# Windowed attention ahead of two expert layers: one chunk of 32 queries with its own 64 keys, in place of two chunks with a shared window of 96

## The chip, the core and the metric

The kernel runs on one core of a Trainium2 chip. Its time is the device time of one execution in microseconds (us). Matrix products run on TensorE (PE in the rows; PEld is its weight load), elementwise work on VectorE (DVE), ScalarE (ACT) and GpSimd (POOL), and transfers are issued by SyncE's queue (SP).

## The reference

Attention looks at a window: 32 queries share 16 keys before them, their own 32 and 8 behind them, and 8 memory keys that all chunks of a batch have. The result goes through two feed-forward layers.

```python
batch, n_heads, seq, head_dim = 4, 8, 768, 64
chunk, left_ctx, right_ctx = 32, 16, 8
for c in range(seq // chunk):
    l_start, r_end = max(0, c*32 - 16), min(seq, c*32 + 40)
    k_full = concat([mem_k, k[:, :, l_start:r_end]])      # 8 + up to 56 keys
    v_full = concat([mem_v, v[:, :, l_start:r_end]])
    scores = (q_c @ k_full.T) / sqrt(64); scores -= max(scores)
    a = exp(scores); out_c = (a / (sum(a) + 1e-9)) @ v_full
x = out.reshape(3072, 512)
x = softplus(x @ w_in) @ w_out                            # 512 -> 2048 -> 512
out = ((x @ w_a) * (x @ w_b)) @ w_out2                    # 512 -> 1536 -> 512
```

## The kernel before, in words

The 3072 tokens are eight tiles of 384. For each tile the attention output `x` is written as a sum of two fp32r halves (high and low), and the first layer walks over 16 slices of 128 hidden units: twelve matmuls into `ph` (L538), softplus on ACT (L544 to L546) and DVE (`g`, L548), the split of `g` (`g_..h` on ACT L525, `g_..l` on DVE L528), and twelve matmuls into `px` (L561), two slices behind. The second layer (L725, L748) follows behind all tiles.

Attention is put between these matmuls. Tile 0 is done before the first `ph`, as six `Block`s of 64 queries that are pipelined over rounds (11 to 37 us), while SP loads and ACT and DVE convert the weights (`raw` L116, `w` L127 and L130). Tiles 1 to 7 take three `Unit`s of 128 queries each (u = 3 to 23), placed between the matmuls of the tile before by a table of due slots. A unit's steps are

- `turn`: 32x32 transposes on DVE bring keys and queries to `kt` and `qt` (L410 to L413), and ACT copies the 8 memory keys behind them (L415);
- `scores`: 32 products of 64 queries with 96 keys (L429), on four 64x64 pieces of the array, into two PSUM banks `sc`;
- `soft`: per head a DVE custom operation (mask, scale, minimum; L379) and an ACT exp with its sum (L383); `norm` on POOL;
- `flip` and `flip2`: ten 32x32-block transposes on DVE (L447) into the one tile `af`;
- `values`: 16 products with contraction 96 on two array pieces, into one PSUM bank `pxa` (L476), each of them 64 queries;
- `place`: ACT copies `pxa` to the high half of `x` (L483), DVE subtracts it from `pxa` for the low half (L484).

Units 3 to 5 (tile 1) differ: their keys come packed from tile loads (scores in pieces of 88 and 8 columns, L304 and L305, or 96 at L302), and `flip_p` transposes on PE through two banks and two ACT copies (L465, L466). The `Block`s have the same steps (scores L302, PE transposes L355, values L363 into `pxb`, place L369 and L370).

`pxa`, `sc` and the transposes' banks take turns in one pool of two PSUM banks named "att": the second `sc` bank of a unit is the bank that the `pxa` two allocations earlier held, so it waits for the place that reads it. PE's, DVE's and SP's orders are written by hand; ACT's and POOL's are the scheduler's from tile 1 on. On SP, a transfer waits for the one eight issues ahead of it. A matmul record with fp32 operands stands twice in the trace for each product.

Of the kernel before, what the change touches and what calls it, by code (L numbers as in the profile page):

```python
# [50 lines left out]
def attn_moe_moe2(ctx: ExitStack, tc: tile.TileContext, q, k, v, mem_k, mem_v,  # L51
# [16 lines left out]
    KS = KB // 32  # L68
    NTILE = NT // TT
    KT = DM // P  # L70
    NF1 = F1 // P
# [80 lines left out]

    def consts():
        make_identity(nc, ident)
        for i, m in enumerate(masks):
            nc.vector.memset(m, NEG)
            for w in range(2):
                for c in range(2):
                    r = slice(QB * w + CH * c, QB * w + CH * c + CH)
                    lo = CH * c + (LC if (i == 3 or (i == 0 and w == 0)) and c == 0 else 0)  # L160
                    hi = CH * c + LC + CH + RC - (RC if (i == 2 and w == c == 1) else 0)
                    nc.vector.memset(m[r, lo:hi], 0.0)
                    nc.vector.memset(m[r, CTX:KB], 0.0)

    NP = TT // 32

# [34 lines left out]

    class Values:
        def __init__(self, name):
            self.v = ap.tile([KB, 2, H, D], F32, name=f"vn{name}")
            self.b = None

        def fetch(self, b, n):
            vv = v[b].rearrange("h s d -> s h d")
            go = nc.sync.dma_start
            for w in range(2):  # L210
                r0 = QU * n - LC + QB * w
                lo, hi = max(r0, 0), min(r0 + CTX, S)
                go(self.v[lo - r0:hi - r0, w], vv[lo:hi])
                if lo > r0:
                    go(self.v[0:lo - r0, w], vv[0:lo - r0])
                if hi < r0 + CTX:
                    go(self.v[hi - r0:CTX, w], vv[2 * hi - r0 - CTX:hi])
                if self.b != b:
                    go(self.v[CTX:KB, w], mem_v[b].rearrange("h m d -> m h d"))
            self.b = b  # L220

    mem_n = ap.tile([P, KT, 32], F32, name="mem_n")
# [6 lines left out]
    for x in (1, 3):  # L229
        nc.gpsimd.memset(af[0:32, x], 0.0)  # L230

    xt = {}

# [8 lines left out]
    class Packed:  # L242
# [66 lines left out]
    class Block:  # L309
# [9 lines left out]
        def load(self):  # L319
            u = self.u  # L320
            if u % 2 == 0:
                first["v"] = wp.tile([P, 2, H, D], F32, tag="w", name=f"vv{u}")
            self.vn = t = first["v"][:KB, u % 2]
            s0 = QB * u - LC
            lo = max(s0, 0)
            go = nc.sync.dma_start
            go(t[lo - s0:CTX], v[0, :, lo:s0 + CTX, :].rearrange("h s d -> s h d"))
            if lo > s0:
                go(t[0:lo - s0], v[0, :, 0:lo - s0, :].rearrange("h s d -> s h d"))
            go(t[CTX:KB], mem_v[0].rearrange("h m d -> m h d"))  # L330

        def scores(self):
            u = self.u
            work = wp.tile([P, 1024], F32, tag="w", name=f"work{u}")
            self.sm = work[:, :KT * KB].rearrange("p (i k) -> p i k", i=KT)
            self.st = work[:, KT * KB:KT * KB + 4 * KT].rearrange("p (n i) -> p n i", n=4)
            sc = self.psum(2, "scb")[:, :KT * KB].rearrange("p (i k) -> p i k", i=KT)
            for i in range(KT):
                for j in range(2):
                    r = slice(64 * j, 64 * j + 64)  # L340
                    packed[0].scores(sc[r, i], i, r, QB * u)
            self.sc = sc

        def soft(self):
# [4 lines left out]

        def flip(self):  # L350
            u = self.u
            self.af = wp.tile([KB, KT, P], F32, tag="w", name=f"afb{u}")
            pa = self.psum(3, "pat")[:KB, :].rearrange("p (i t) -> p i t", i=KT)
            for i in range(KT):
                nc.tensor.transpose(pa[:, i], self.sm[:, i], ident)  # L355
            nc.scalar.copy(self.af, pa)

        def values(self):
            self.px = px = self.psum(4, "pxb")[:, :KT * QB].rearrange("p (i t) -> p i t", i=KT)
            for i in range(KT):  # L360
                for j in range(2):
                    r = slice(64 * j, 64 * j + 64)
                    nc.tensor.matmul(px[r, i], lhsT=self.vn[:, 2 * i + j, :], rhs=self.af[:, i, r], start=True, stop=True)  # L363

        def place(self):
            u = self.u
            x = x_tile(0)
            xh, xl = x[:, 0, :, u * QB:u * QB + QB], x[:, 1, :, u * QB:u * QB + QB]
# [23 lines left out]
    class Unit:  # L392
# [10 lines left out]
        def turn(self):  # L403
            u, kn, qn = self.u, loaded.k, loaded.q
            n0 = 4 * (u % UPT)
            if self.n == 0:
                nc.vector.transpose(out=mem_t, in_=mem_n)
            self.kt = a2.tile([P, KT, 2, KB], F32, tag="kt", name=f"kt{u}", bufs=1)
            self.qt = a2.tile([P, KT, QU], F32, tag="qt", name=f"qt{u}", bufs=1)
            nc.vector.transpose(out=self.kt[:, :, :, :64].rearrange("p i w (m s) -> p i w m s", m=2),  # L410
                                in_=kn[:, :, n0:n0 + 4].rearrange("p i (w m) d -> p i w m d", m=2))
            nc.vector.transpose(out=self.kt[:, :, :, 64:], in_=kn[:, :, n0 + 2:n0 + 5:2])
            nc.vector.transpose(out=self.qt, in_=qn[:, :, n0:n0 + 4].rearrange("p i n d -> p i (n d)"))  # L413
            for w in range(2):
                nc.scalar.copy(self.kt[:, :, w, CTX:], mem_t[:, :, :M])  # L415

        def scores(self):
            u = self.u
# [2 lines left out]
            for i in range(KT):  # L421
                for j in range(2):
                    r = slice(64 * j, 64 * j + 64)
                    for w in range(2):
                        c = slice(QB * w, QB * w + QB)
                        if u < 2 * UPT:
                            packed[1].scores(self.sc[j][c, i], i, r, QU * (u - UPT) + QB * w)
                            continue
                        nc.tensor.matmul(self.sc[j][c, i], lhsT=self.qt[r, i, c], rhs=self.kt[r, i, w],  # L429
                                         start=True, stop=True)  # L430

        def soft(self):
# [9 lines left out]

        def flip(self, pieces=(0, 1)):

            for x in pieces:
                for kb in range(x % 2, KS):
                    nc.vector.transpose(out=af[32 * kb:32 * kb + 32, x],  # L447
                                        in_=self.sm[32 * x:32 * x + 32, :, 32 * kb:32 * kb + 32])

        def flip2(self):  # L450
            self.flip((2, 3))
# [7 lines left out]

        def flip_p(self):  # L460

            for j in range(2):
                pa = ps.tile([P, 512], F32, tag="att", name=f"pa{j}_{self.u}")[:KB].rearrange("p (i t) -> p i t", i=KT)
                for i in range(KT):
                    nc.tensor.transpose(pa[:, i], self.sm[:, KT * j + i], ident)  # L465
                nc.scalar.copy(af[:, :, KT * j:KT * j + KT], pa.rearrange("p i (x s) -> p x i s", x=4))  # L466

        def values(self):
            u = self.u
            vn = self.v.v  # L470
            self.px = px = ps.tile([P, 512], F32, tag="att", name=f"pxa{u}").rearrange("p (i t) -> p i t", i=KT)

            for w in range(2):
                for i in range(KT):
                    for j in range(2):
                        nc.tensor.matmul(px[64 * j:64 * j + 64, i, QB * w:QB * w + QB], lhsT=vn[:, w, 2 * i + j],  # L476
                                         rhs=af[:, 2 * w:2 * w + 2, KT * j + i], start=True, stop=True)

        def place(self):
            t, c0 = divmod(self.u * QU, TT)  # L480
            x = x_tile(t)
            xh, xl = x[:, 0, :, c0:c0 + QU], x[:, 1, :, c0:c0 + QU]
            nc.scalar.copy(xh, self.px)  # L483
            nc.vector.tensor_tensor(xl, self.px, xh.bitcast(F32), ALU.subtract)  # L484

    def warm(n, what=ident):

# [541 lines left out]
```

## Time and profile before

| | before |
|---|---|
| time, median of 3 runs (range) | 1198.33 us (1197.76 to 1199.57) |
| profiled execution | 1196.18 us, span 1194.1 us |
| PE busy | 1180.2 us (99% of the span) |
| PEld busy | 1120.6 us (94%) |
| DVE busy | 736.9 us (62%) |
| ACT busy | 536.3 us (45%) |
| POOL busy | 279.3 us (23%) |
| DMA | 209.86 MB, mean 176 GB/s |

The busy times are sums over the span; a PE that is 99% busy says that nearly every change on PE's path shows in the time, and that the others wait for it. The profiled execution lies 2.15 us below the median of the runs, 2.08 us of it outside the span.

### The profile page before, as it was taken

To read this page: it belongs to the slowest core of one execution; us is meant where nothing else is said; L and a number is where in the kernel's file an instruction comes from. 1 tells how busy PE (TensorE), PEld (TensorE's weight loads), DVE (VectorE), ACT (ScalarE), POOL (GpSimd) and SP (SyncE) were. 2 spreads that over 40 slices of the span, in tenths; PEclk is the share of its full clock that TensorE was granted. 3 is DMA by queue.
4 is the path that set the end of the run, shared out by engine and by line. 5 is a ranking of instruction groups with operands and counts; after the bars stand their busy time and mean duration, and the time that the engine had idled before them with its cause. 6 is when DMAs were issued, how large, how long until landed. Compare 5 with 4: busy or idle time off the path is not lost.

```text
span 1194.1 us, 21573 instructions
## 1 busy us (share of the span) xinstructions
PE 1180.2 (99%) x7994; PEld 1120.6 (94%) x7994; DVE 736.9 (62%) x1706; ACT 536.3 (45%) x1329; POOL 279.3 (23%) x249
## 2 busy tenths in 40 slices
PE   8999999999999999999999999999999999999998
PEld 8899999999999999999999999999999999999997
DVE  7888654556545565455387677755656456655565
ACT  6898656665566666566564433211112211212110
POOL 1000322323223222232325878200211002100000
PEclk9999999999999999999999999999999999999999
DMA  9955244352443534432465895788554965379521
GB/s 238 300 168 107 81 109 101 108 102 86 109 97 111 102 92 103 111 95 66 149 231 208 324 342 199 267 316 308 202 197 142 373 232 182 129 265 364 185 77 54
DMA packets 198697, 209.86 MB, mean 176 GB/s; under 512 B 121616, under 2 KB 149952, under 8 KB 198592
## 3 DMA queue, kind: packets, MB, share of 16 engines
q1 hardware_dynamic: 198208, 208.43, 54.7%
q8 instruction: 63, 1.03, 0.4%
q14 instruction: 42, 0.34, 0.1%
q0 software_dynamic: 384, 0.05, 0.0%
HBM read 158.11 MB, written 50.33 MB: 175 GB/s over the span
## 4 chain that ended last, share of the span: by engine, by line
PE 89%; DVE 3%; ACT 3%; DMA 2%; SPq 1%; issue 1%; DVEq 0%; ACTq 0%
PE ph L538 20%; PE px L561 20%; PE py L748 17%; PE pW L725 8%; PE pV L725 8%; PE pX L725 8%; PE pY L725 4%; PE pxa L476 2%; PE sc L429 1%; DMA kp<-in_k_dram 1%; DVE af L447 1%; DMA raw<-in_moe_w_in_dram 1%; ACT sm L383 1%; SPq L330 1%; DVE g L548 1%
## 5 line engine op out<-in xcount | busy, mean ns | idle before, releaser
L538 PE MATMUL ph<-x,w 128*128 128x384 f32 x1536 | 289.7, 336 | 0.1
L538 PEld LDWEIGHTS ph<-x,w 128*128 128x128 f32 x1536 | 267.0, 188 | 2.4 <-issue 0.3
L748 PE MATMUL py<-w2o,c 128*128 128x512 f32 x864 | 222.9, 394 | 0.7 <-DVE c L818 0.5
L548 DVE SCALAR_TENSOR_TENSOR g<-ph,e 128x384 f32<-128x384 f32 x128 | 71.3, 557 | 206.7 <-ACT e L546 198.8
L748 PEld LDWEIGHTS py<-w2o,c 128*128 128x128 f32 x864 | 159.9, 188 | 26.8 <-DVE c L818 1.1
L807 ACT CAST c<-c 128x384 fp32r<-128x384 f32 x48 | 24.7, 514 | 303.9 <-DVE c L805 271.2
L725 PE MATMUL pX<-x,u 128*128 128x384 f32 x576 | 115.5, 334 | 0.0
L757 DVE TENSOR_TENSOR y<-py,y 128x512 f32<-128x512 f32 x120 | 82.9, 691 | 48.2 <-PE py L748 47.8
L544 ACT ACTIVATE e<-ph 128x384 f32<-128x384 f32 x128 | 62.3, 486 | 102.3 <-PE ph L538 86.5
L725 PEld LDWEIGHTS pX<-x,u 128*128 128x128 f32 x576 | 102.1, 188 | 4.1
L447 DVE STREAM_TRANSPOSE af<-sm 32x256 f32<-32x256 f32 x180 | 78.2, 435 | 2.6
L545 ACT ACTIVATE e<-e 128x384 f32<-128x384 f32 x128 | 67.3, 526 | 4.0
L803 DVE TENSOR_TENSOR d<-pW,q 128x384 f32<-128x384 f32 x48 | 26.7, 557 | 68.4 <-PE pW L725 68.4
L546 ACT ACTIVATE e<-e 128x384 f32<-128x384 f32 x128 | 67.3, 526 | 3.7
L383 ACT ACTIVATE sm<-sm,st 128x96 f32<-128x96 f32 x168 | 60.5, 361 | 4.9 <-DVE st L379 4.9
L817 ACT CAST c<-c 128x384 fp32r<-128x384 f32 x48 | 24.6, 513 | 77.8 <-DVE c L815 76.9
L725 PE MATMUL pW<-xs,u 128*128 128x384 f32 x288 | 57.8, 335 | 0.0
L725 PE MATMUL pV<-xx,u 128*128 128x384 f32 x288 | 57.8, 335 | 0.0
L725 PE MATMUL pW<-xx,u 128*128 128x384 f32 x288 | 57.6, 334 | 0.0
L725 PE MATMUL pY<-xs,u 128*128 128x384 f32 x288 | 57.6, 334 | 0.0
L725 PE MATMUL pV<-xs,u 128*128 128x384 f32 x288 | 57.6, 334 | 0.0
L725 PEld LDWEIGHTS pV<-xx,u 128*128 128x128 f32 x288 | 51.5, 188 | 4.1
(251 smaller groups left out, 2240.0 us busy)
## 6 DMA issues: line engine op xcount, KB each, us to landing
u<-u_scratch SPq DMA_DIRECT2D x108, 512.0 KB
u_scratch<-u SPq DMA_DIRECT2D x36, 512.0 KB
w2o<-w2o_scratch SPq DMA_DIRECT2D x36, 512.0 KB
u<-u_scratch SPq DMA_DIRECT2D x36, 256.0 KB
raw<-in_moe_w_in_dram SPq DMA_DIRECT2D x16, 512.0 KB
raw<-in_moe_w_out_dram SPq DMA_DIRECT2D x16, 512.0 KB
vn<-in_v_dram SPq DMA_DIRECT2D x35, 176.0 KB
raw_a<-in_moe_w_a_dram SPq DMA_DIRECT2D x12, 512.0 KB
```

The lines of the kernel that those rows point to most:

```text
L383: nc.scalar.activation(sm[:, h], sm[:, h], AF.Exp, bias=st[:, 0, h:h + 1], scale=-1.0, accum_out=st[:, 1, h:h + 1])
L447: nc.vector.transpose(out=af[32 * kb:32 * kb + 32, x], in_=self.sm[32 * x:32 * x + 32, :, 32 * kb:32 * kb + 32])
L538: nc.tensor.matmul(ph, lhsT=a, rhs=c, start=n == 0, stop=n == 3 * KT - 1)
L544: nc.scalar.activation(e, ph, AF.Abs)
L545: nc.scalar.activation(e, e, AF.Exp, scale=-1.0)
L546: nc.scalar.activation(e, e, AF.Ln, bias=1.0)
L548: nc.vector.scalar_tensor_tensor(g, ph, 0.0, e, ALU.max, ALU.add)
L561: nc.tensor.matmul(acc[t][i][:, :TT], lhsT=a, rhs=c, start=f == 0 and m == 0, stop=f == NF1 - 1 and m == 2)
L725: nc.tensor.matmul(bank[:, :TT], lhsT=u[:, j, a, kt * P:kt * P + P], rhs=x[:, c, kt, :], start=first_ and m == 0, stop=m == 3 * KH - 1, sk ...
L748: nc.tensor.matmul(b, lhsT=c[:, x, r], rhs=w[:, y], start=n == 0, stop=n == 3 * GROUP - 1)
L757: tt(y, b, y, ALU.add)
L803: tt(d21, w[:, :TT], q, ALU.add)
```

## The change

Chunks of 32 queries get their own 56 keys and the 8 memory keys, 64 in all, where two chunks shared 88 and 8. A score product has 32 queries and 64 columns, on 64x32 pieces of the array, eight of them; a unit has 32 products instead of 16 (64 records instead of 32). A value product has contraction 64 in the upper or the lower half of the array and 32 queries; the halves go to two PSUM banks, `pxa` and `pxb`, and `place` is two copies and two subtractions of 256 columns instead of one each of 512. Values are loaded per chunk (56 rows) and so overlap more. The PE transposes become products with columns of the identity, into one bank. The masks lose most of their work, since a chunk's own window needs no hole.

```diff
-    CTX = QB + LC + RC
+    CTX = CH + LC + RC
     KB = CTX + M
+    NC = QU // CH
...
-            self.v = ap.tile([KB, 2, H, D], F32, name=f"vn{name}")
+            self.v = ap.tile([P, 2, H, D], F32, name=f"vn{name}")
...
-            for w in range(2):
-                r0 = QU * n - LC + QB * w
+            for g in range(NC):
+                x, y = divmod(g, 2)
+                r0 = QU * n - LC + CH * g
...
-    af = ap.tile([KB, 4, H, 32], F32, name="af")
+    af = ap.tile([P, H, 2, CH], F32, name="af")
...
-            lhsT = self.q[i][r, s0:s0 + QB]
+            lhsT = self.q[i][r, s0:s0 + CH]
...
-            go(t[lo - s0:CTX], v[0, :, lo:s0 + CTX, :].rearrange("h s d -> s h d"))
...
-            go(t[CTX:KB], mem_v[0].rearrange("h m d -> m h d"))
+            for c in range(2):
+                s0 = QB * u + CH * c - LC
...
+                go(t[to + lo:to + s0 + CTX], v[0, :, lo:s0 + CTX, :].rearrange("h s d -> s h d"))
...
+                go(t[KB * c + CTX:KB * c + KB], mem_v[0].rearrange("h m d -> m h d"))
...
-                nc.tensor.transpose(pa[:, i], self.sm[:, i], ident)
+                for c in range(2):
+                    nc.tensor.matmul(pa[KB * c:KB * c + KB, i], lhsT=self.sm[:, i], rhs=one[:, c], start=True, stop=True)
...
-            nc.vector.transpose(out=self.kt[:, :, :, :64].rearrange("p i w (m s) -> p i w m s", m=2),
-                                in_=kn[:, :, n0:n0 + 4].rearrange("p i (w m) d -> p i w m d", m=2))
-            nc.vector.transpose(out=self.kt[:, :, :, 64:], in_=kn[:, :, n0 + 2:n0 + 5:2])
+            for m in (1, 0):
+                nc.vector.transpose(out=self.kt[:, :, :, 32 * m:32 * m + 32], in_=kn[:, :, n0 + m:n0 + m + NC])
...
-            for w in range(2):
-                nc.scalar.copy(self.kt[:, :, w, CTX:], mem_t[:, :, :M])
+            nc.scalar.copy(self.kt[:, :, :, CTX:],
+                           mem_t[:, :, :M].rearrange("p i (o m) -> p i o m", o=1).to_broadcast([P, KT, NC, M]))
...
-                    for w in range(2):
-                        c = slice(QB * w, QB * w + QB)
+                    for g in range(NC):
+                        c = slice(CH * g, CH * g + CH)
...
-            for x in pieces:
-                for kb in range(x % 2, KS):
...
+            for g in pieces:
+                for kb in range(2):
...
-            for j in range(2):
-                pa = ps.tile([P, 512], F32, tag="att", name=f"pa{j}_{self.u}")[:KB].rearrange("p (i t) -> p i t", i=KT)
...
+            pa = ps.tile([P, 512], F32, tag="att", name=f"pa{self.u}").rearrange("p (h x s) -> p h x s", h=H, x=2)
...
-            self.px = px = ps.tile([P, 512], F32, tag="att", name=f"pxa{u}").rearrange("p (i t) -> p i t", i=KT)
...
+            self.px = [ps.tile([P, 512], F32, tag="att", name=f"px{'ab'[y]}{u}")[:, :KT * QB].rearrange(
+                "p (i x s) -> p i x s", i=KT, x=2) for y in range(2)]
...
-                        nc.tensor.matmul(px[64 * j:64 * j + 64, i, QB * w:QB * w + QB], lhsT=vn[:, w, 2 * i + j],
-                                         rhs=af[:, 2 * w:2 * w + 2, KT * j + i], start=True, stop=True)
+                    for y in range(2):
+                        k = slice(KB * y, KB * y + KB)
+                        for j in range(2):
+                            nc.tensor.matmul(self.px[y][64 * j:64 * j + 64, i, x], lhsT=vn[k, x, 2 * i + j],
+                                             rhs=af[k, KT * j + i, x], start=True, stop=True)
...
-            nc.scalar.copy(xh, self.px)
-            nc.vector.tensor_tensor(xl, self.px, xh.bitcast(F32), ALU.subtract)
+            x = x_tile(t)[:, :, :, c0:c0 + QU].rearrange("p n i (x y s) -> p n y i x s", x=2, y=2)
+            for y in range(2):
+                xh, xl = x[:, 0, y], x[:, 1, y]
+                nc.scalar.copy(xh, self.px[y])
+                nc.vector.tensor_tensor(xl, self.px[y], xh.bitcast(F32), ALU.subtract)
```

PE takes its blocks in the same order as before. Three places show how the other engines' orders move. The first is ACT around the place of unit 7, in tile 2's preparation, where `e_10` and `g_10h` belong to slice 10, `kt` to unit 8 and `raw_b` to a weight of the second layer. Before:

```order
217 L544 ACTIVATE e_10_2333<-ph_10_2320 128x384
218 L545 ACTIVATE e_10_2333<-e_10_2333 128x384
219 L415 COPY kt_2313<-mem_t 128x4x8 x2
220 L546 ACTIVATE e_10_2333<-e_10_2333 128x384
221 L483 CAST x_2093<-pxa_2343 128x4x128
222 L525 CAST g_10h<-g_10_2337 128x384
223 L635 ACTIVATE raw_b_2270<-raw_b_2270 128x512
224 L544 ACTIVATE e_11_2431<-ph_11_2418 128x384
```

And of the change, in the same place:

```order
224 L554 ACTIVATE e_10_2730<-ph_10_2717 128x384
225 L418 COPY kt_2711<-mem_t 128x16x8
226 L555 ACTIVATE e_10_2730<-e_10_2730 128x384
227 L556 ACTIVATE e_10_2730<-e_10_2730 128x384
228 L493 CAST x_2473<-pxa_2740 128x4x2x32
229 L535 CAST g_10h<-g_10_2734 128x384
230 L645 ACTIVATE raw_b_2669<-raw_b_2669 128x512
231 L493 CAST x_2473<-pxb_2741 128x4x2x32
232 L554 ACTIVATE e_11_2865<-ph_11_2852 128x384
```

The memory keys' copy stands ahead of two of the three softplus steps, and the second half of the place, from `pxb`, stands behind the split of `g` and a weight's conversion, not beside the first half.

The second place is DVE at the same point; `af` is the transposed softmax of unit 7. Before:

```order
373 L548 SCALAR_TENSOR_TENSOR g_9_2290<-ph_9_2273,e_9_2286 128x384
374 L447 STREAM_TRANSPOSE af<-sm_2151 32x256 x5
375 L410 STREAM_TRANSPOSE kt_2313<-kn 128x8x64
376 L412 STREAM_TRANSPOSE kt_2313<-kn 128x8x32
377 L413 STREAM_TRANSPOSE qt_2314<-qn 128x512
378 L548 SCALAR_TENSOR_TENSOR g_10_2337<-ph_10_2320,e_10_2333 128x384
379 L484 TENSOR_TENSOR x_2093<-pxa_2343,x_2093 128x4x128
```

And of the change:

```order
352 L558 SCALAR_TENSOR_TENSOR g_9_2689<-ph_9_2672,e_9_2685 128x384
353 L452 STREAM_TRANSPOSE af<-sm_2551 32x8x32 x4
354 L416 STREAM_TRANSPOSE kt_2711<-kn 128x16x32 x2
355 L417 STREAM_TRANSPOSE qt_2712<-qn 128x512
356 L558 SCALAR_TENSOR_TENSOR g_10_2734<-ph_10_2717,e_10_2730 128x384
357 L494 TENSOR_TENSOR x_2473<-pxa_2740,x_2473 128x4x2x32
358 L494 TENSOR_TENSOR x_2473<-pxb_2741,x_2473 128x4x2x32
```

One transpose of `af` less, a longer second `kt` transpose, and the one subtraction is two.

The third place is SP while the blocks' values and the first weights are loaded (`vv` are the values of blocks 2 and 3). Before:

```order
14 L101 DMA raw_155<-in_moe_w_in_dram 128x4x256
15 L327 DMA vv_157<-in_v_dram 88x8x64
16 L330 DMA vv_157<-in_mem_v_dram 8x8x64
17 L101 DMA raw_160<-in_moe_w_out_dram 128x1024
```

And of the change:

```order
18 L101 DMA raw_129<-in_moe_w_in_dram 128x4x256
19 L325 DMA vv_131<-in_v_dram 56x8x64
20 L328 DMA vv_131<-in_mem_v_dram 8x8x64
21 L325 DMA vv_131<-in_v_dram 56x8x64
22 L328 DMA vv_131<-in_mem_v_dram 8x8x64
23 L101 DMA raw_136<-in_moe_w_out_dram 128x1024
```

Between two weights four transfers of values stand where two stood, with 128 rows of 2 KB in place of 96.

## Rows read from the trace of the kernel before

**Rows 1.** The page: the chain that ended last, share by engine
```profile
PE 89%; DVE 3%; ACT 3%; DMA 2%; SPq 1%; issue 1%; DVEq 0%; ACTq 0%
```

**Rows 2.** Windows: PE, PEld, DVE, ACT, POOL busy, PEclk, DMA share, GB/s
```profile
16.00:22.00 6.00, 5.28 (x76) 4.70 (x75) 5.63 (x26) 5.11 (x22) 0.00 (x0) 1.00 1.00 238
...
93.00:97.00 4.00, 4.00 (x18) 3.60 (x16) 3.09 (x7) 3.61 (x7) 0.00 (x0) 0.57 0.77 183
```

**Rows 3.** The chain and ACT's timeline at the end of tile 0's attention
```profile
30.15 10.18 DMA raw<-in_moe_w_in_dram
...
40.35 0.71 ACT L116 ACTIVATE raw<-raw 128x512 f32<-128x512 f32 x1 [0.75 <-DMA raw<-in_moe_w_in_dram]
```

**Rows 4.** Timelines of ACT and PE at the end of tile 1's attention
```profile
90.89 1.04 ACT L466 COPY af<-pa 96x512 f32<-96x512 f32 x2
...
91.50 0.33 PE L476 MATMUL pxa<-af,vn 96*64 96x64 f32 x2 [1.34 <-ACT af L466]
91.99 1.15 PE L476 MATMUL pxa<-af,vn 96*64 96x64 f32 x30 [0.15 <-ACT af L466]
```

**Rows 5.** PE's timeline in a block's round
```profile
24.51 0.69 PE L363 MATMUL pxb<-afb,vv 96*64 96x64 f32 x16
...
25.77 0.88 PE L302 MATMUL scb<-kt,qt 64*64 64x96 f32 x16
```

**Rows 6.** PE's timeline, scores of unit 3 in pieces of 88 and 8 columns
```profile
53.21 0.40 PE L304 MATMUL sc<-kn,qn 64*64 64x88 f32 x8
53.40 0.28 PE L305 MATMUL sc<-kn,qn 64*64 64x8 f32 x8
53.48 0.41 PE L304 MATMUL sc<-kn,qn 64*64 64x88 f32 x8
```

**Rows 7.** PE's timeline, scores and values of two later units
```profile
198.73 0.89 PE L429 MATMUL sc<-kt,qt 64*64 64x96 f32 x32
...
218.48 1.15 PE L476 MATMUL pxa<-af,vn 96*64 96x64 f32 x32
```

**Rows 8.** Waits of PE: what for, us in total, times, longest us
```profile
PE pxa L476 <- DVE af L447: 1.6, 2, 1.1
...
PE sc L429 <- DVE x L484: 0.5, 1, 0.5
```

**Rows 9.** Timelines of PE, ACT and DVE around the place of unit 7
```profile
169.82 1.22 PE L476 MATMUL pxa<-af,vn 96*64 96x64 f32 x32
170.98 0.45 PE L561 MATMUL px<-g_8h,w 128*128 128x384 f32 x1
...
173.26 1.10 PE L429 MATMUL sc<-kt,qt 64*64 64x96 f32 x32
...
171.41 0.34 ACT L415 COPY kt<-mem_t 128x32 f32<-128x32 f32 x2 [0.43 <-DVE kt L412]
172.08 0.57 ACT L483 CAST x<-pxa 128x512 fp32r<-128x512 f32 x1
172.86 0.51 ACT L525 CAST g_10h<-g 128x384 fp32r<-128x384 f32 x1 [0.22 <-DVE g L548]
173.28 0.70 ACT L635 ACTIVATE raw_b<-raw_b 128x512 f32<-128x512 f32 x1
...
168.07 2.24 DVE L447 STREAM_TRANSPOSE af<-sm 32x256 f32<-32x256 f32 x5
170.34 0.71 DVE L410 STREAM_TRANSPOSE kt<-kn 128x512 f32<-128x512 f32 x1
170.97 0.40 DVE L412 STREAM_TRANSPOSE kt<-kn 128x256 f32<-128x256 f32 x1
172.75 0.68 DVE L484 TENSOR_TENSOR x<-pxa,x 128x512 fp32r<-128x512 f32 x1
```

**Rows 10.** ACT's and DVE's timelines: a block's place, of 256 columns
```profile
23.08 0.36 ACT L369 CAST x<-pxb 128x256 fp32r<-128x256 f32 x1
...
23.48 0.42 DVE L370 TENSOR_TENSOR x<-pxb,x 128x256 fp32r<-128x256 f32 x1
```

More of the change, by code (lines that the diff above doesn't have):

```diff
@@ L67, in attn_moe_moe2 @@
     BPT = TT // QB
-    KS = KB // 32
     NTILE = NT // TT
@@ L154, in consts @@
         make_identity(nc, ident)
-        for i, m in enumerate(masks):
-            nc.vector.memset(m, NEG)
-            for w in range(2):
[L158 to L163, printed above, removed]
+        for m in masks:
+            nc.vector.memset(m, 0.0)
+        for i, c in ((0, 0), (3, 0), (3, 2)):
+            nc.vector.memset(masks[i][CH * c:CH * c + CH, 0:LC], NEG)
+        nc.vector.memset(masks[2][QU - CH:QU, CTX - RC:CTX], NEG)
     NP = TT // 32
@@ L340, in scores @@
                     r = slice(64 * j, 64 * j + 64)
-                    packed[0].scores(sc[r, i], i, r, QB * u)
+                    for c in range(2):
+                        o = 64 * j + CH * c
+                        packed[0].scores(sc[o:o + CH, i], i, r, QB * u + CH * c)
             self.sc = sc
@@ L351, in flip @@
             u = self.u
-            self.af = wp.tile([KB, KT, P], F32, tag="w", name=f"afb{u}")
-            pa = self.psum(3, "pat")[:KB, :].rearrange("p (i t) -> p i t", i=KT)
+            self.af = wp.tile([P, KT, 2, CH], F32, tag="w", name=f"afb{u}")
+            pa = self.psum(3, "pat")[:, :KT * QB].rearrange("p (i j s) -> p i j s", i=KT, j=2)
+            one = ident.rearrange("p (j c s) -> p c j s", j=2, c=2)
             for i in range(KT):
-                nc.tensor.transpose(pa[:, i], self.sm[:, i], ident)
+                for c in range(2):
+                    nc.tensor.matmul(pa[KB * c:KB * c + KB, i], lhsT=self.sm[:, i], rhs=one[:, c], start=True, stop=True)
             nc.scalar.copy(self.af, pa)
         def values(self):
-            self.px = px = self.psum(4, "pxb")[:, :KT * QB].rearrange("p (i t) -> p i t", i=KT)
+            self.px = [self.psum(4, f"px{'ab'[c]}")[:, :KT * CH].rearrange("p (i t) -> p i t", i=KT) for c in range(2)]
             for i in range(KT):
-                for j in range(2):
-                    r = slice(64 * j, 64 * j + 64)
-                    nc.tensor.matmul(px[r, i], lhsT=self.vn[:, 2 * i + j, :], rhs=self.af[:, i, r], start=True, stop=True)
+                for c in range(2):
+                    k = slice(KB * c, KB * c + KB)
+                    for j in range(2):
+                        nc.tensor.matmul(self.px[c][64 * j:64 * j + 64, i], lhsT=self.vn[k, 2 * i + j, :],
+                                         rhs=self.af[k, i, j], start=True, stop=True)
         def place(self):
-            u = self.u
             x = x_tile(0)
-            xh, xl = x[:, 0, :, u * QB:u * QB + QB], x[:, 1, :, u * QB:u * QB + QB]
-            nc.scalar.copy(xh, self.px)
-            nc.vector.tensor_tensor(xl, self.px, xh.bitcast(F32), ALU.subtract)
+            for c in range(2):
+                s = QB * self.u + CH * c
+                xh, xl = x[:, 0, :, s:s + CH], x[:, 1, :, s:s + CH]
+                nc.scalar.copy(xh, self.px[c])
+                nc.vector.tensor_tensor(xl, self.px[c], xh.bitcast(F32), ALU.subtract)
     first = {}
@@ L423, in scores @@
                     r = slice(64 * j, 64 * j + 64)
-                    for w in range(2):
-                        c = slice(QB * w, QB * w + QB)
+                    for g in range(NC):
+                        c = slice(CH * g, CH * g + CH)
                         if u < 2 * UPT:
-                            packed[1].scores(self.sc[j][c, i], i, r, QU * (u - UPT) + QB * w)
+                            packed[1].scores(self.sc[j][c, i], i, r, QU * (u - UPT) + CH * g)
                             continue
-                        nc.tensor.matmul(self.sc[j][c, i], lhsT=self.qt[r, i, c], rhs=self.kt[r, i, w],
+                        nc.tensor.matmul(self.sc[j][c, i], lhsT=self.qt[r, i, c], rhs=self.kt[r, i, g],
                                          start=True, stop=True)
@@ L443, in flip @@
         def flip(self, pieces=(0, 1)):
-            for x in pieces:
-                for kb in range(x % 2, KS):
-                    nc.vector.transpose(out=af[32 * kb:32 * kb + 32, x],
-                                        in_=self.sm[32 * x:32 * x + 32, :, 32 * kb:32 * kb + 32])
+            for g in pieces:
+                for kb in range(2):
+                    o = KB * (g % 2) + 32 * kb
+                    nc.vector.transpose(out=af[o:o + 32, :, g // 2],
+                                        in_=self.sm[CH * g:CH * g + CH, :, 32 * kb:32 * kb + 32])
         def flip2(self):
@@ L460, in flip_p @@
         def flip_p(self):
-            for j in range(2):
-                pa = ps.tile([P, 512], F32, tag="att", name=f"pa{j}_{self.u}")[:KB].rearrange("p (i t) -> p i t", i=KT)
-                for i in range(KT):
-                    nc.tensor.transpose(pa[:, i], self.sm[:, KT * j + i], ident)
-                nc.scalar.copy(af[:, :, KT * j:KT * j + KT], pa.rearrange("p i (x s) -> p x i s", x=4))
+            pa = ps.tile([P, 512], F32, tag="att", name=f"pa{self.u}").rearrange("p (h x s) -> p h x s", h=H, x=2)
+            one = ident.rearrange("p (x y s) -> p y x s", x=2, y=2)
+            for h in range(H):
+                for y in range(2):
+                    nc.tensor.matmul(pa[KB * y:KB * y + KB, h], lhsT=self.sm[:, h], rhs=one[:, y], start=True, stop=True)
+            nc.scalar.copy(af, pa)
         def values(self):
```

32 lines of the change are left out of this document (14 added, 18 removed).

## The prediction

> **What bounds the kernel now.** I read the page's busy times first: PE is busy for 99% of the span. The chain that ended last puts 89% on PE and some 3% each on DVE and ACT [rows 1]; following it in order of time, that remainder lies in the first 98 us. Then the windows and timelines, stretch by stretch. Up to 37 us transfers fill the queue: 238 GB/s at a DMA share of 1.00, with no engine busy for the whole window [rows 2]; one transfer of weights holds 10.18 us of the chain, and behind it an ACT conversion stands 0.75 us for its weight [rows 3]. From there to 92 us ACT and DVE convert the remaining weights and do tile 1's softmax, and their chain ends where PE stands 1.34 us and then 0.15 for the two ACT copies of unit 5's transposes [rows 4]. Behind that the granted clock is 0.57 from 93 to 97 us [rows 2], nearer 1.2 than 2.4 GHz. From 98 us on PE itself is the bound: a step counts by what it occupies of PE, or by PE standing for it, and in the list of PE's waits little stands there [rows 8].
>
> **The price of a product.** 16 value records on two array pieces make a row of 0.69 us [rows 5], 32 a row of 1.15 [rows 7]: 0.46 us for eight more rounds, 58 ns for a round of 64 columns. Scores of 96 columns: 16 records on two pieces make 0.88 us [rows 5], 32 on four 0.89 [rows 7]. Twice the pieces did twice the work in the same time, and eight rounds of 96 columns cost 0.20 more than eight of 64, so a round of 96 takes 58 + 25 = 83 ns. Where rounds of 88 and of 8 columns alternate, two of each take 53.48 - 53.21 = 0.27 us [rows 6]; two of 88 columns, at 77 ns between the two prices, leave 0.12, 58 ns for a round of 8 columns. A round of few columns is no cheaper than one of 64.
>
> **Scores.** The change makes 64 records on eight pieces: eight rounds of 64 columns, 0.69 instead of 0.89 us, if eight run together as four did. That is -0.20 for each of 18 units (u = 6 to 23), **-3.6**. If only four run together, there are 16 rounds, 1.15, +0.26 each, +4.7. No row shows eight pieces; I take -3.6, for the doubling that rows do show was free.
>
> **Values.** A piece has eight products before and after, so 16 rounds, now of 32 columns on four pieces. At the 58 ns that 8 and 64 columns both cost: **0**. The bound below is half a round's price, -0.46 each, -8.3; the bound above is zero, since four pieces of this size do run together in the scores before [rows 7].
>
> **Values that wait for the flips.** Before, ten DVE transposes of 0.45 us each (five take 2.24 [rows 9]); now eight, so each half ends 0.45 earlier and both 0.9. PE stands for them twice, 1.6 us in all, 1.1 the longest [rows 8]: 0.9 and 0.5 of that go. Besides, 13 value blocks run 0.07 to 0.19 us over the 1.08 from their start to the next instruction (unit 7's: 169.82 to 170.98, 1.16 [rows 9]), 1.1 us in all, which go too. **-2.5**; bounds -2.7 and -1.4 (the short ones stay).
>
> **The place of units 7, 10 and 13.** These are the middle units of tiles 2, 3 and 4; here the next unit's scores come one `px` group behind the values, and their second bank is the one that the place must have read. Before, the scores row is 1.10 us instead of 0.89: PE stands 0.2 there already [rows 9]. Now: the flips end 0.45 earlier, and the second `kt` transpose takes 0.71 instead of 0.40, so ACT's memory copy, which waits for it, ends at about 171.45 instead of 171.65. But it now stands ahead of two softplus steps and not one, so the copy of `pxa` begins at about 172.45 instead of 172.08 [rows 9]. It takes 0.36 [rows 10] instead of 0.57, then come `g_10h` (173.2) and `raw_b` (173.6), since the copy of `pxb` was put behind both. With 0.57 us for `raw_b` from start to next start it begins at 174.2, takes 0.36; the subtraction adds 0.1 and 0.42 [rows 10]: 175.1. PE comes at 173.2. Queued behind its scores are the twelve `ph` matmuls of the next slice, whose softplus ACT and DVE take up next. PE stands 1.9 us less the 0.2 of before: 1.7 each, **+5.1**. Bounds: 0 if the copy of `pxb` finds ACT free earlier, +6 if the whole of `raw_b` is paid. In tiles 5 to 7 the order is the same, but the scores follow 5.5 us behind the values, which covers it. The 0.5 us of PE's other wait for a place [rows 8] belongs to unit 6 and stays.
>
> **The early transfers.** Six blocks load 64 KB more each, 384 KB; at 238 GB/s [rows 2] that is 1.65 us, and the 10.18 us transfer [rows 3] ends so much later, which ACT's conversion at 40.35 pays in full, as it stands for its weight already. I take **+1.7**; bounds 0 (if the transfers before had slack) and +3.4 (if many small rows cost twice). Within the blocks' rounds two short chains take the place of one, two PSUM banks are asked for instead of one, and DVE has some 0.2 us less per round; this ends in front of the last weight, which covers it.
>
> **From 46 to 98 us.** Sixteen exps lose 32 columns at (0.57 - 0.36)/256 us a column [rows 9, 10], -0.4; one copy of transposes instead of two, -0.5 (half of 1.04 [rows 4]); places in two pieces, +0.2: PE gets its values 0.7 earlier. The second half's wait with the split it makes, 91.50 to 91.99 [rows 4], is gone, -0.5, and unit 6's scores are 0.2 shorter. The PE transposes as 16 products have 16 rounds, +0.3, under PE's waiting. **-1.4**; bounds -3.1 (if the clock's fall, which cost about 1.7, goes as well) and 0.
>
> **What costs nothing.** Masks are set before the first load lands; POOL, 23% busy, normalises a third fewer columns; SP's additional loads from tile 2 on lie under a DMA share far from 1.
>
> **Sum.** -3.6 + 0 - 2.5 + 5.1 + 1.7 - 1.4 = -0.7: 1196.18 - 0.7 = 1195.5 for a profiled execution. The profiled one lies 2.15 below the median of the runs, so **1197.6** there. 0.2%, 2.4 us, is about what a measurement of this kernel can tell from no change.
>
> **Rivals.** *The clock falls after the new waits.* After the standing of 1.34 us at 91.5 the granted clock went to 0.57 [rows 2, 4]; after the one of 1.1 us in [rows 8] it stayed at full. Three standings of 1.9 us could each do it, at 1.7 us more: -0.7 + 3.4 = +2.7 for two, +4.4 for three, 1201.0 to 1202.7, slower. It decides from two falls on.
>
> *The place wait does not come about:* -0.7 - 5.1 = -5.8, 1192.5, faster. For it: PE is late by other work, or ACT is ahead by then. Against: ACT's order is fixed, and the replay above has 1.9 us to lose.
>
> *Eight pieces do not run together:* +0.46 x 18 = +8.3, 1205.9, slower. Against: four did.
>
> *Value products of 32 columns are cheaper than 58 ns:* -8.3, 1189.3, faster. Against: 8 columns cost as much as 64 [rows 6].
>
> *The early transfers are covered:* -1.7, 1195.9, at the bound of faster.
>
> *Evacuation is the price, not the order.* Every later unit pays two copies and two subtractions: (2 x 0.36 - 0.57) + (2 x 0.42 - 0.68) = 0.31 us [rows 9, 10], 18 times, 5.6 in place of 5.1: 1198.1. The Trainium skill, "TensorEngine Tiling (Array Packing)", section "PSUM Bottleneck", says that tiling speeds TensorE up but not the emptying of PSUM, and advises one access over several tiles of a bank; this change goes against that advice. The trace speaks against its price here: ACT is 45% busy and DVE 62%.
>
> **How the numbers follow.** The sum as it stands 0.38, the clock 0.17, no place wait 0.15, eight pieces apart 0.08, cheap values 0.08, transfers covered or evacuation 0.14. Faster: 0.15 + 0.08 + 0.07 of the transfers + 0.03 of the sum = 0.33; slower: 0.17 + 0.08 + 0.02 = 0.27; same 0.40. The range takes in the clock's three falls and the missing place wait, 1192.3 to 1202.7, and leaves out both array cases, 0.16. The likeliest case's own range is 1195.5 to 1200.
>
> **What would show it.** Right: scores of a later unit as a row of about 0.69 us; values 1.15; PE standing some 1.9 us before the second half of the scores near 173, 247 and 322 us, put down to the subtraction L494; ACT's conversion near 41 us standing longer than 0.75; the two waits for the flips shrunk. Wrong: a scores row above 1 us without a wait, values near 0.7, a granted clock below 1.00 after 98 us, or places that PE does not wait for.

## The result, and the profile after

The change is slower: 1205.76 us, median of 9 runs (1202.49 to 1210.22), against 1199.49 for the kernel before (9 runs, 1197.76 to 1200.36). The ratio is 1.0056, with a 95% interval of 1.0039 to 1.0073, so 5 to 9 us. Forecast were 1197.6 and no difference, with a range up to 1202.7. The profiled execution took 1202.49 us, its span is 1200.6, 6.5 above that of before. One execution of one kernel below, twice, took 3146 us at a granted clock of 1.00, with PE's products more than twice as long throughout, and is left out of its ratio.

The page: busy times, the chain's shares and, of the queue that the trace names "instruction", packets, MB and share.

```profile
PE 1183.5 (99%) x9866; PEld 1121.0 (93%) x9866; DVE 717.2 (60%) x1669; ACT 530.9 (44%) x1335; POOL 270.8 (23%) x247
...
PE 92%; ACT 3%; DVE 3%; issue 1%; DVEq 0%; POOL 0%; POOLq 0%
...
q8 instruction: 78, 1.28, 0.5%
```

DVE, ACT and POOL all have less to do than before, and PE is busy for only 3.3 us more, 2.3 of them in `ph` (292.0 against 289.7 us), whose matmuls are as many as before; the rows on the end of each tile show a wait inside them. The other 3.2 us are PE idle. Transfers have gone from the chain [rows 1]. So most of the 6.5 us is PE standing, and not more work. PE's waits, with what for, us in total, times and the longest:

```profile
PE scb L300 <- issue: 4.4, 3, 3.1
PE sc L433 <- DVE x L494: 3.4, 4, 1.0
PE sc L300 <- DVE x L494: 1.6, 1, 1.6
```

The waits for the flips [rows 8] are gone, and two kinds have grown: scores of the blocks that wait for nothing the profile shows ("issue"), and scores that wait for a place. A third kind stands only in the list of PE's weight loads, below.

To see where the time comes in, I set the same pieces of PE's order side by side in both traces. The first `ph` begins at 41.53 instead of 37.41, 4.1 later; at the first `ph` behind unit 5's scores (101.73 against 98.57) it is 3.2; behind the last unit's values, 6.9; at the end 6.5. So the first 40 us lose 4.1, the stretch from there to 100 us gives back 1.0, and tiles 1 to 6 lose 3.8.

**The first 40 us.** PE's timeline in the scores of block 1, in two later places, and the first `ph`:

```profile
13.03 0.25 PE L301 MATMUL scb<-kt,qt 64*32 64x8 f32 x5
16.35 0.27 PE L300 MATMUL scb<-kt,qt 64*32 64x56 f32 x4 [3.08 <-issue]
...
26.21 0.27 PE L300 MATMUL scb<-kt,qt 64*32 64x56 f32 x4 [0.80 <-issue]
...
36.07 0.24 PE L366 MATMUL pxa<-afb,vv 64*64 64x32 f32 x1 [0.36 <-issue]
...
41.53 2.61 PE L548 MATMUL ph<-x,w 128*128 128x384 f32 x12
```

And in the kernel before:

```profile
15.70 0.17 PE L305 MATMUL scb<-kt,qt 64*64 64x8 f32 x1 [0.77 <-issue]
...
37.41 2.66 PE L538 MATMUL ph<-x,w 128*128 128x384 f32 x12
```

The 3.08 us stand in the middle of block 1's scores, between two products of like operands. The kernel before stands for "issue" in the same stretch too, but 0.77 us. Behind the change's standing the granted clock is near 1.2 GHz for 4 us, which the kernel before does not have there (1.00 from 13 to 30 us); PE's windows of the change (length, PE busy, granted clock, DMA share, GB/s):

```profile
17.00:19.00 2.00, 2.00 (x68) 0.59 0.90 197
19.00:21.00 2.00, 2.00 (x12) 0.56 0.95 276
21.00:24.00 3.00, 3.00 (x112) 1.00 0.99 260
```

**The end of each tile.** ACT, DVE, PE and PE's weight loads where unit 8's place and the first `ph` of tile 2 meet (unit 8 is the last of that tile):

```profile
200.07 0.51 ACT L535 CAST g_15h<-g 128x384 fp32r<-128x384 f32 x1 [0.69 <-DVE g L558]
200.49 0.37 ACT L493 CAST x<-pxa 128x256 fp32r<-128x256 f32 x1
200.75 0.38 ACT L493 CAST x<-pxb 128x256 fp32r<-128x256 f32 x1
...
201.23 0.41 DVE L494 TENSOR_TENSOR x<-pxb,x 128x256 fp32r<-128x256 f32 x1
...
201.18 2.70 PE L548 MATMUL ph<-x,w 128*128 128x384 f32 x12
...
201.18 0.19 PEld L548 LDWEIGHTS ph<-x,w 128*128 128x128 f32 x1 [0.41 <-ACT x L493]
201.70 1.34 PEld L548 LDWEIGHTS ph<-x,w 128*128 128x128 f32 x8 [0.33 <-DVE x L494]
```

The next tile's `ph` reads all of `x`. It waits first for the copy, then for the subtraction. By the starts of the blocks on PE this costs 0.7 us in each of the six tiles 2 to 7: 0.25 in front of the `ph` and 0.46 inside its row. In the kernel before the copy of `pxa` stood ahead of `g_15h`, and the same `ph` took 2.25 us and waited for nothing:

```profile
194.83 0.57 ACT L483 CAST x<-pxa 128x512 fp32r<-128x512 f32 x1
195.62 0.51 ACT L525 CAST g_15h<-g 128x384 fp32r<-128x384 f32 x1 [0.22 <-DVE g L548]
...
196.56 2.25 PE L538 MATMUL ph<-x,w 128*128 128x384 f32 x12
```

**The place of unit 7,** and scores of a later unit that waits for nothing:

```profile
174.20 0.30 ACT L418 COPY kt<-mem_t 128x128 f32<-128x128 f32 x1 [0.23 <-DVE kt L416]
...
175.39 0.35 ACT L493 CAST x<-pxa 128x256 fp32r<-128x256 f32 x1
...
176.59 0.67 ACT L645 ACTIVATE raw_b<-raw_b 128x512 f32<-128x512 f32 x1
177.16 0.35 ACT L493 CAST x<-pxb 128x256 fp32r<-128x256 f32 x1
...
176.73 0.32 PE L433 MATMUL sc<-kt,qt 64*32 64x64 f32 x8
178.02 0.79 PE L433 MATMUL sc<-kt,qt 64*32 64x64 f32 x56 [0.98 <-DVE x L494]
...
203.81 0.86 PE L433 MATMUL sc<-kt,qt 64*32 64x64 f32 x64
204.60 0.44 PE L571 MATMUL px<-g_14h,w 128*128 128x384 f32 x1
```

The wait that the prediction replayed is there, in units 7, 10 and 13, but it is 0.98 long, and 1.29 from the first of the scores, where the replay had 1.9. And the 64 records of a unit's scores (32 products) take 0.79 us to the next instruction, hardly less than the 0.82 of the 32 records (16 products) before.

### The profile page after: what moved, and what is told of

It is laid out like the page before. It is cut to its first block, busy times and chain, and to the rows that moved or that the text cites. A ratio compares the mean times of both kernels' runs of the same rounds, so it can differ in the third digit from the quotient of the medians.

```text
span 1200.6 us, 25431 instructions
## 1 busy us (share of the span) xinstructions
PE 1183.5 (99%) x9866; PEld 1121.0 (93%) x9866; DVE 717.2 (60%) x1669; ACT 530.9 (44%) x1335; POOL 270.8 (23%) x247
## 4 chain that ended last, share of the span: by engine, by line
PE 92%; ACT 3%; DVE 3%; issue 1%; DVEq 0%; POOL 0%; POOLq 0%
PE ph L548 21%; PE px L571 19%; PE py L758 17%; PE pV L735 8%; PE pW L735 8%; PE pX L735 8%; PE pY L735 4%; PE sc L433 1%; PE fill L502 1%; DVE g L558 1%; ACT e L556 1%; ACT e L555 1%; PE pxa L485 1%; DVE af L452 1%; ACT e L554 1%
## 5 line engine op out<-in xcount | busy, mean ns | idle before, releaser
L548 PE MATMUL ph<-x,w 128*128 128x384 f32 x1536 | 292.0, 337 | 1.0
L767 DVE TENSOR_TENSOR y<-py,y 128x512 f32<-128x512 f32 x120 | 82.8, 690 | 48.6 <-PE py L758 48.2
L452 DVE STREAM_TRANSPOSE af<-sm 32x256 f32<-32x256 f32 x144 | 62.6, 435 | 2.7
L388 ACT ACTIVATE sm<-sm,st 128x64 f32<-128x64 f32 x168 | 56.0, 335 | 4.5 <-DVE st L384 4.5
```

The lines of the kernel that those rows point to most:

```text
L388: nc.scalar.activation(sm[:, h], sm[:, h], AF.Exp, bias=st[:, 0, h:h + 1], scale=-1.0, accum_out=st[:, 1, h:h + 1])
L452: nc.vector.transpose(out=af[o:o + 32, :, g // 2], in_=self.sm[CH * g:CH * g + CH, :, 32 * kb:32 * kb + 32])
L548: nc.tensor.matmul(ph, lhsT=a, rhs=c, start=n == 0, stop=n == 3 * KT - 1)
L767: tt(y, b, y, ALU.add)
```

## The experiments

Spans are those of the profiled executions, ratios those of the timed runs to the kernel before. Two theories stood against each other at each end. For the first 40 us: PE waits for its own longer instruction stream; or the larger value loads delay the blocks. For the rest: ACT's new order; or the price of emptying two banks, wherever it stands.

**place_first.** ACT takes a unit's two copies ahead of the split of `g`; the weight conversions (`raw_b`) that are due there are held back behind the split:

```diff
-                    emit_soft(t, f, ph)
+                    emit_soft(t, f, ph, place=partial(att_at, 2 * (NF1 * t + f)))
...
+            place()
+            copy = placed.pop()
+            with tc.issue_after(copy.ins) if copy else ExitStack():
+                gt[t, f] = split(g, f"g{t}_{f}", engine, two)
```

> The changed kernel, with the two copies of a unit's place put on ACT ahead of the split of the slice's g, as in the kernel before; PE's and DVE's orders stay. Theory (ACT's order costs the time from 98 us on): the first ph of tiles 2 to 7 no longer stands some 0.6 us for the place of the last unit, and the scores behind units 7, 10 and 13 stand some 0.6 us instead of 1.2: 6 x 0.6 + 3 x 0.6 = 5.4 us off, span about 1195 instead of 1200.6. The first 98 us stay as long as in the changed kernel. Rival (emptying two banks costs 0.3 us a unit wherever it stands): at most 1 us off.

Span 1195.4, 5.2 less than the change's, and ratio 1.0002 (0.9986 to 1.0018), 6.5 us less by the ratios. ACT and PE at the same two places:

```profile
199.63 0.36 ACT L493 CAST x<-pxa 128x256 fp32r<-128x256 f32 x1
199.88 0.38 ACT L493 CAST x<-pxb 128x256 fp32r<-128x256 f32 x1
200.42 0.52 ACT L537 CAST g_15h<-g 128x384 fp32r<-128x384 f32 x1 [0.16 <-DVE g L562]
...
201.28 2.24 PE L550 MATMUL ph<-x,w 128*128 128x384 f32 x12
...
178.24 0.92 PE L433 MATMUL sc<-kt,qt 64*32 64x64 f32 x64
```

The `ph` is back at 2.24 us, and the scores behind unit 7 stand 0.06 us instead of 0.98 + 0.25. The evacuation is as long as in the change; only ACT's order is another. So the order is the cause, and the price of the evacuation is out as a rival.

**old_blocks** and **both.** The six blocks of tile 0 as in the kernel before (64 queries, masks of 96 columns), in the change and in place_first:

```diff
+    CTXB = QB + LC + RC
+    KBB = CTXB + M
...
+                    packed[0].scores(sc[r, i], i, r, QB * u, QB)
```

> The changed kernel, with the six blocks of tile 0 as before: 64 queries, 96 keys, values loaded as 88 and 8 rows. Theory (the first 98 us lose time because PE stands for its own longer instruction stream in the blocks' scores): the first ph begins 3 to 4 us earlier than in the changed kernel and the span is about 1197. Rival (the blocks' end is covered by the weights' transfers, and the loss is in units 3 to 5): less than 1 us off.

> Both edits, place first and the old blocks. If the two losses are separate, the sum: 5.4 + 3.5 = 8.9 us off the changed kernel, span about 1191.5, some 2.5 us below the kernel before. If they overlap, or the shorter stretch meets another wait, between 1193 and 1196.

old_blocks: span 1197.8, first `ph` at 37.88, ratio 1.0022 (1.0013 to 1.0031), 4.1 us less than the change. both: span 1192.2, ratio 0.9966 (0.9956 to 0.9977). By the ratios the two edits take off 6.5 and 4.1 us alone and 10.8 together: two separate losses, as the sum of the two theories had it, and together they are more than all that the change lost. What is left of the change gains some 4 us.

**fewer_loads, one_product, loads, twice** take the blocks' loss apart: transfers or instructions.

```diff
 # fewer_loads, of the change
+            nc.gpsimd.memset(t[KB:P], 0.0)
-            for c in range(2):
+            for c in range(1):
 # one_product, of the change
-            if s0 + CTX == m0:
+            if s0 + CTX == m0 or self.t == 0:
 # loads, of the kernel before
+            go(more[:24], v[0, :, QB * u:QB * u + 24, :].rearrange("h s d -> s h d"))
+            go(more[24:], mem_v[0].rearrange("h m d -> m h d"))
 # twice, of the kernel before
+                    for _ in range(2):
                         packed[0].scores(sc[r, i], i, r, QB * u)
```

> The changed kernel, with no value loads for the second chunk of each block: those rows are zeros written by GpSimd, so half of tile 0's values are left out. Fewer bytes and no more transfers than in the kernel before, the PE instructions of the changed kernel. Instruction stream: the standing of about 3 us near 13 to 16 us stays, and the first ph begins at 40.5 us or later. Transfers: the first ph goes back to 37.5 to 38.5 and the span falls by 3 us or more.

> The changed kernel, with one score product of 64 columns a head and chunk in tile 0, where 56 and 8 columns take two: the 8 memory keys are left out there and the next 8 tokens stand in their place. The transfers of the changed kernel, 96 products fewer on PE ahead of the first ph. Instruction stream: the standing near 13 us falls below 1.5 us, and the first ph begins at 39 us or before. Transfers: the first ph stays at 41 us or later.

> The kernel before, with 24 and 8 rows of values more per block loaded to rows that nothing reads: the transfers' number and bytes of the changed kernel's blocks, PE as before. Theory (instruction stream): the first ph stays within 0.5 us of 37.4 and the span within 1 us. Rival (the value loads delay the blocks): the first ph 3 to 4 us later. The sum of the prediction has 1.7 later, at the weights' conversion behind 40 us.

> The kernel before, with each score product of the six blocks issued twice into the same columns: as many PE instructions there as in the changed kernel, same transfers, same values. Theory (PE stands for its own longer instruction stream in the blocks): a standing put down to no engine of 2 to 3 us near 11 to 16 us, and the first ph begins 3 to 4 us later than 37.4. Rival (the larger value loads delay the blocks): the first ph moves by the products' own 1.0 us or less, most of it covered.

> The kernel before with the blocks' score products issued twice, once more for its profile, since the first one was taken in an execution of 3146 us in which PE's products took more than twice as long throughout. Instruction stream: a standing put down to no engine of 2 to 3 us near 11 to 16 us, and the first ph 3 to 4 us later than 37.4. Transfers: 38.5 us or before.

PE's timelines of fewer_loads (two rows) and of one_product (one):

```profile
15.87 0.32 PE L300 MATMUL scb<-kt,qt 64*32 64x56 f32 x3 [3.09 <-issue]
...
28.31 0.19 PE L301 MATMUL scb<-kt,qt 64*32 64x8 f32 x1 [2.00 <-issue]
```

```profile
15.45 0.31 PE L298 MATMUL scb<-kt,qt 64*32 64x64 f32 x6 [1.08 <-issue]
```

With fewer bytes than before the standing is still 3.09 us; with the bytes of the change and fewer products (88 by the records) it falls to 1.08, and the first `ph` begins at 38.38. So the standing goes with PE's instructions, not with the value loads. fewer_loads' own time says nothing on the loads: after its two standings the granted clock was 0.59 from 30 to 45 us, its first `ph` came at 48.2, and its ratio is 1.0087.

one_product shows the transfers as well. Its ratio, 1.0043 (1.0028 to 1.0058), is hardly better than the change's: of the 3.2 us that it is ahead at the first `ph` 1.7 are lost at once, where ACT waits 2.02 us for a weight and PE 1.56 for the query copy behind it:

```profile
42.49 0.71 ACT L116 ACTIVATE raw<-raw 128x512 f32<-128x512 f32 x1 [2.02 <-DMA raw<-in_moe_w_in_dram]
...
48.52 0.88 PE L289 MATMUL ptq<-ident,qp 128*64 128x128 f32 x12 [1.56 <-DVE qn L291]
```

Of the rest, part goes near 61 us, where PE stands 0.64 us for "issue" again, and part in a fall of the clock (0.50 from 102 to 105 us) that the change's execution does not have, so its span does not give the sum.

loads: the first `ph` begins at 41.58, as the rival had it, while PE stands for "issue" only twice, 0.96 us at 9.5 (in the transposes of the keys) and 0.57 in the blocks. But the profiled execution is the longest of its ten runs, 1203.83 us; the shortest is 1197.94, and the ratio, 1.0010 (0.9999 to 1.0022), 1.2 us, is not clear of no change. Its 24 rows a block went slowly, one transfer 9.3 us, so the pattern is harsher than the change's. So larger loads can delay the blocks. In the change itself they do not show: its chain up to the first `ph` is PE's work, its standing for "issue" and 1.0 us of other engines, with no transfer in it. That they cost something where the blocks are on time is shown by one_product, 1.7 us; how much of the change's 4.1 is theirs beside the standing is not shown.

twice missed: its ratio is 1.0042 and the first `ph` of its profile (twice_again) begins at 41.78, as the theory had it, but there is no standing. The doubled products stretch a block's scores to 2.69 us instead of 1.19 (they write the same columns), which by itself makes the rounds longer, and there are 658 records ahead of the first `ph`, not the change's 842. That execution reaches the critical instruction late, and so waits 0.2 us there. The next paragraph says which instruction that is.

**What PE stands for.** I counted PE's records from the start. In the kernel before, the change, place_first, halves, fewer_loads, one_product and loads, the standing is at record 221 or 222, whichever block and product that is. The trace's transfer records have one fetch of 16 KB on the instruction queue shortly before: in the change from 13.61 to 14.68, and PE goes on at 16.35. The kernel before: landed 14.19, on at 15.70; place_first 14.05 and 15.63; fewer_loads 14.42 and 15.87; one_product 14.01 and 15.45. In all seven PE goes on 1.3 to 1.7 us behind the landing, at 15.2 to 17.3 us. What differs is when PE gets there: 14.7 in the kernel before, 13.1 in the change, whose products are shorter and more (842 records ahead of the first `ph` instead of 482). old_blocks gets there at 15.4, 1.4 behind its landing, and does not stand. The change has five fetches between 12 and 36 us against three, and PE stands again at records 474, 601 and 726 (26.2, 30.5 and 36.1 us), each time 1.3 to 1.6 behind a landing and two, one and one steps of some 126 records further on. Nor is it the kernel's start alone: in halves PE stands 2.35 us at 288.2, 1.4 behind a landing, in the middle of a unit's scores. The trace does not name the engine that a fetch is for; that it is PE's is argued from these records and times.

```profile
q1 hardware_dynamic: 1554, 0.79, 101.4%
q8 instruction: 1, 0.02, 2.1%
```

That is the change's transfer view from 13.2 to 16.4 us (queue, packets, MB, share of the engines' time): the one fetch lies among value and weight packets that fill the queues.

**halves.** Each score product of the later units in two of 32 columns:

```diff
+                        for n in (slice(0, 32), slice(32, 64)):
-                        nc.tensor.matmul(self.sc[j][c, i], lhsT=self.qt[r, i, c], rhs=self.kt[r, i, g],
+                            nc.tensor.matmul(self.sc[j][c, i, n], lhsT=self.qt[r, i, c], rhs=self.kt[r, i, g, n],
```

> The changed kernel, each score product of units 6 to 23 in two of 32 columns: 64 products where 32 stood, the same columns in all. If a product's pace is set by the instructions that it takes, whatever its columns, the scores last 0.16 + 2 x 0.63 = 1.4 us instead of 0.79, +0.6 for each of 18 units, +11 us. If it is set by the columns that go through the eight pieces, they stay near 0.8.

Span 1217.2, one execution; a unit's scores (median) last 1.39 us. First those of unit 6, then a row of PE's waits:

```profile
133.63 1.45 PE L434 MATMUL sc<-kt,qt 64*32 64x32 f32 x128 [0.22 <-DVE qt L417]
135.00 0.44 PE L572 MATMUL px<-g_15h,w 128*128 128x384 f32 x1
...
PE sc L434 <- issue: 2.4, 1, 2.4
```

32 products more of half the columns cost 0.60 us, 19 ns each. 32 x 19 ns + 0.16 = 0.77 is what the change's scores take. So a product here has a price of its own, whether it has 64 columns or 32. Each product also loads its own weights, and halves doubles those loads too (128 records instead of 64), so whether the price is the product's issue or its weight load is open. The span is 16.6 us above the change's and not 11: the scores make 10.7, the first `ph` comes 1.9 later, PE stands 2.4 once for "issue", and the granted clock is 0.54 for 3 us behind that.

**both_later.** The scores of unit 5 one slot later, in both:

```diff
-               ((20.9, "scores"), (21, "weigh"), (26, "flip_p"), (27.9, "values"), (28, "place")))
+               ((21.9, "scores"), (22, "weigh"), (26, "flip_p"), (27.9, "values"), (28, "place")))
```

> The faster version (place first and the old blocks), with unit 5's scores one slot later, behind the next ph. Theory (those scores stand 1.6 us for the place of unit 4, and the granted clock falls behind that standing): both go, 1.6 and up to 1.7 us, span 1189 to 1190.6 instead of 1192.2. Rival (ACT's softmax of unit 5, now later, makes its transposes or values stand instead): no gain, or some loss, between 1192 and 1194.

Ratio 0.9938 (0.9924 to 0.9952): 7.4 us below the kernel before, the fastest of all, and 3.4 below both by the ratios. First both, where those scores stand, then both_later:

```profile
96.78 0.26 PE L311 MATMUL sc<-kn,qn 64*32 64x56 f32 x3 [1.63 <-DVE x L498]
```

```profile
98.39 0.51 PE L552 MATMUL ph<-x,w 128*128 128x384 f32 x2
98.83 0.26 PE L311 MATMUL sc<-kn,qn 64*32 64x56 f32 x3
```

The standing is gone, and the granted clock stays at 1.00 there. The 3.4 us are what the theory had (1.6 and 1.7). Its profiled span, 1191.8, misses the forecast of 1189 to 1190.6: in that execution PE waits 1.72 us near 48 us, for the query copy that stands behind a weight's conversion.

## Why the prediction was wrong

**Scores, -3.6: wrong.** "0.69 instead of 0.89 us, if eight run together as four did", which is 0.62 from start to next start, measured 0.79, -0.03 a unit and not -0.20, -0.6 in all. The rival, four at once, was wrong as well. The step priced rounds, from rows of 16 and 32 records with 2 and 4 pieces at work; with 64 records on eight pieces the number of products sets the pace, 19 ns each (halves). 3.0 us of the miss.

**Values, 0: nearly right.** 1.06 instead of 1.08 to 1.15.

**The flips, -2.5: right.** The waits of 1.1 and 0.5 us are gone and the short ones too. Value blocks of units 6 to 23 sum to 3.5 us less, values and flips together. Some of it is this execution's luck: with the same flips place_first waits 0.6 us once and old_blocks 0.5.

**The place of units 7, 10 and 13, +5.1: right in mechanism, too large.** The order and its stop behind `raw_b` are as foretold; each scores block takes 2.02 us instead of 1.02, so +3.0. The replay had ACT's memory copy wait for both `kt` transposes. It waits for the first alone, which brings its upper columns: it begins 0.8 us behind the start of the values and not 1.4, and the copy of `pxa` 2.0 behind and not 2.6 (174.20 and 175.39 against values at 173.38). All that follows is 0.6 earlier.

**The last unit of each tile: not in the sum.** This is the step that failed most: a term put at nothing without a reason. The prediction looked at ACT's order at the middle units only, and said nothing of the last ones. There not scores but the next tile's `ph` waits for the place, and ACT's order changed at that point too, with the copies behind `g_15h`. Six times 0.7 us, 4.3. It could have been read ahead of the run, from the same order of ACT.

**The early transfers, +1.7: wrong in place and cause.** The loss was to fall on ACT's conversion near 41 us, behind the first `ph`. There ACT waits for no weight any more. The blocks ended 4.1 us later, ahead of the first `ph`, and not for their loads first of all but for PE's instructions (3.08 us instead of 0.77, three shorter standings of 0.80, 0.48 and 0.36, and the clock's fall behind the first), on which the sum had nothing. That the last weight covers what the blocks' rounds lose could hold only as long as these ended on time. The weights do land later by the trace's records of landings, as reckoned: the transfer of 10.18 us [rows 3] 1.25 us later in the change, those after it 1.3 to 1.7. In the change that lies behind the blocks' delay. Where the delay is less it comes out: in one_product the same weight lands 2.1 us later, and ACT waits for it.

**46 to 98 us, -1.4:** -1.0, and near the number by luck. The 1.34 us for two copies and the second wait are gone, and so is the fall of the clock behind them. The prediction took them for unit 5's; by PE's order they are unit 4's, and what follows is unit 5's scores, which need unit 4's place. PE comes to them earlier and stands 1.62 us there. And the scores and PE transposes of units 3 and 4 take 1.0 us more in all, of which the sum had nothing. What the step missed is what is late next.

Together: 6.5 = 4.1 - 1.0 + 3.8 - 0.4 behind the last tile. The last stretch's 3.8 are 4.3 for the tiles' ends, 3.0 for the three places, -3.5 for values, -0.6 for scores, 0.3 for unit 5's longer transposes and 0.3 at unit 6's scores, which wait for its transposed queries. Against the forecast of -0.7 that is 7.2 more: +4.3 at the tiles' ends, +3.0 in the scores and +2.4 in the blocks, against -2.1 at the three places and -1.0 in values and flips; the rest is small. Of the rivals, the clock's fall did come, but behind the standing in the blocks and not behind the three places, where it stays at 1.00. The rule of the Trainium skill that the prediction cites ("TensorEngine Tiling (Array Packing)", section "PSUM Bottleneck") says that tiling does not speed up the emptying of PSUM. The trace agrees that PE came to wait for that, but the length of the emptying is not the cause: with the same two copies taken earlier by ACT the 6.5 us are gone (place_first).

## What to carry to other kernels

Where a change splits a step in two, read the scheduler's order of every engine at every place where that step is awaited, the end of a tile among them, and not only where a wait already shows. Count a change's instructions as well as its columns: on eight pieces each product cost PE 19 ns whatever its columns, and where transfers fill the queues PE can run ahead of its own instructions. When a wait goes, look at what the engine meets next: here a place took over from two copies.

## What was not expected of the hardware

PE stands at a fixed instruction, record 221 or 222, until 1.3 to 1.7 us behind the landing of a 16 KB fetch: 0.8 us in the kernel before, 3.1 in the change, and none where it gets there later than that. And the granted clock does not always answer to the same standing. Behind 1.6 us of standing for unit 4's place it went to 0.57 from 101 to 105 us in place_first and to 0.67 from 97 to 101 in both, and stayed at 1.00 in the change and in old_blocks; why is open.

```profile
101.00:105.00 4.00, 4.00 (x108) 0.57 1.04 308
```

```profile
101.00:105.00 4.00, 4.00 (x86) 1.00 1.07 307
```

These are the windows of PE from 101 to 105 us in place_first and in the change: PE's busy time, granted clock, DMA share and GB/s. The clock's varying answer fits the wider spread of the change's runs, 8 us against 3, but no run here ties the two together.
